# Two-part depth sum for an output projection, a half swap on the matrix engine, and a new order of one block's work in a fused attention and FFN kernel

## The chip, the cores and the metric

The kernel runs on one core of a Trainium2 chip. The metric is device microseconds of that core for one execution. The granted TensorE clock was 1.0 or within 0.4% of it. The span of a profile, from its first to its last instruction, is 1.8 to 1.9 us shorter than the time of the same run. A time is the median of several runs; every figure read from a trace is that of one profiled run. Engine names: PE is TensorE's matmul, PEld its weight load, DVE VectorE, ACT ScalarE, POOL GpSimd, SP SyncE.

## The reference

A lightning attention (causal, with a decay per head and a running state) is followed by a gated FFN. Cut to what matters:

```python
# q, k, v: (4, 8, 768, 64);  lam: (8,)
for b in range(nb):                                   # blocks of the sequence
    intra = einsum('bhic,bhjc->bhij', qb, kb) * Dmask         # scores times decay
    intra = einsum('bhij,bhjd->bhid', intra, vb)
    inter = einsum('bhid,bhde->bhie', qb * lam_pow, kv_state)
    out[:, :, sl] = intra + inter
    kv_state = lam_block * kv_state + einsum('bhsd,bhse->bhde', kb * rev_pow, vb)
x = out.transpose(0, 2, 1, 3).reshape(3072, 512)
y = (sigmoid(x @ w_gate) * (x @ w_val)) @ w_out               # 512 -> 1536 -> 512
```

## The kernel before

The sequence is cut into six blocks `n` of 128 positions for all four batches. A block has attention work (transposes `tk`, `tq`; scores `sp`; masked scores `MT`; outputs `op`, copied to `XT`; state sums `cp`, kept in `Sb`, from keys `kd` scaled by their decay) and FFN work: twelve column tiles `ft`, each with a gate product `gp` and a value product `vp`, whose gated result is `ht`, and a projection `po` of four row tiles. PE runs one program: attention of block n+1 is strewn between FFN products of block n, except at the start, where nothing can hide it. Weights arrive through POOL's DMA queue with a cast from float32 to bfloat16, between the loads of q, k and v. The parts that the change touches (cuts marked):

```python
    def load_gv(f0, f1):                       # gate and value weights of some column tiles
        fs = slice(f0 * 128, f1 * 128)
        nc.gpsimd.dma_start(out=WG[:, :, fs], in_=wg_r[:, :, fs])
        nc.gpsimd.dma_start(out=WV[:, :, fs], in_=wv_r[:, :, fs])
    def load_wo(c0, c1):                       # w_out by columns
        nc.gpsimd.dma_start(out=WO[:, :, c0:c1], in_=wo_r[:, :, c0:c1])
    ...
    def swap_halves():                         # the decay with its 64-row halves swapped
        for u in range(2):
            o, i = rows_of(u), rows_of(1 - u)
            nc.scalar.dma_start(out=lamq2[o, 1], in_=lamq2[i, 0])
            nc.scalar.dma_start(out=dec2[o, 1], in_=dec2[i, 0])
    ...
    def piece_po(n, tt, c0, c1, eng):          # projection of one row tile, full depth
        po = ps_ff.tile([128, DM], FP32, name="po", tag="ff")
        for ft in range(NFT):
            nc.tensor.matmul(po[:, :c1 - c0], lhsT=HT[n, ft][:, tt * 128:(tt + 1) * 128],
                             rhs=WO[:, ft, c0:c1], start=(ft == 0), stop=(ft == NFT - 1))
        ...                                    # copied to OB; stored at once if n > 0
    ...
    # end of block 0: projection by column halves, with block 1's attention between
    po(0, 0, m_(1, 1), kd(1, 4, 6, parts=[0]), c=cols[0])
    po(0, 1, pair(piece_c, 0, 0), pair(piece_c, 0, 1), kd(1, 6, 8, parts=[0]), c=cols[0])
    po(0, 2, trans(1, 1), c=cols[0])           # trans: k's and q's transposes together
    po(0, 3, pair(piece_s, 1, 1), m_(1, 2), m_(1, 3), kd(1, 0, 8, parts=[1]), att(1), c=cols[0])
    ...
            more[3].extend([lambda tt=tt: store(0, tt) for tt in range(B)])   # block 0's results
```

In `po(n, tt, *more)` the projection comes first and the listed pieces follow it.

Of the kernel before, what the change touches and what calls it, by code (L numbers as in the profile page):

```python
# [8 lines left out]
FP32 = mybir.dt.float32  # L9
# [7 lines left out]
def kernel(  # L17
# [65 lines left out]
    def load(n, what, b0=0, b1=B):  # L83
        sl = slice(n * C, (n + 1) * C)
        for c in what:
# [9 lines left out]
            if nat < b1:  # L95
                m = max(nat, b0)
                for u in range(2):
                    nc.gpsimd.dma_start(  # L98
                        out=T_[c, n][:, m:b1, u::2, :],
                        in_=src[m:b1, 1 - u::2, sl, :].rearrange("b h s d -> s (b h) d"))  # L100

    def load_gv(f0, f1):
        fs = slice(f0 * 128, f1 * 128)
        nc.gpsimd.dma_start(out=WG[:, :, fs], in_=wg_r[:, :, fs])  # L104
        nc.gpsimd.dma_start(out=WV[:, :, fs], in_=wv_r[:, :, fs])  # L105

    def load_wo(c0, c1):
        nc.gpsimd.dma_start(out=WO[:, :, c0:c1], in_=wo_r[:, :, c0:c1])

    KD = {}  # L110

# [23 lines left out]
    def load_hw(c, b, eng):  # L135
# [12 lines left out]
    nc.vector.memset(neg, 0.0)  # L148
    nc.vector.memset(tri, 0.0)
    make_identity(nc, ident, nomemset=True)  # L150
    nc.gpsimd.iota(dij, pattern=[[1, C]], base=0, channel_multiplier=-1,
                   allow_small_or_imprecise_dtypes=True)
    nc.gpsimd.affine_select(out=neg, in_=neg, compare_op=ALU.is_ge, fill=-30000.0, base=0,
# [13 lines left out]
    load(0, "v", 3, 4)  # L167
    for ft in range(4):
        load_gv(ft, ft + 1)
    load_gv(4, 6)  # L170

    lnl = const.tile([128, H], FP32, tag="lnl")
    nc.scalar.activation(lnl, lam_bc, AF.Ln)
    lnp = const.tile([128, HP], FP32, tag="lnp")
    for u in range(2):
        us = slice(u * 64, (u + 1) * 64)
        nc.scalar.activation(lnp[us, :], lam_bc[us, u::2], AF.Ln)
    lamq2 = const.tile([128, 2, HP, C], BF16, tag="lamq2")
    lamq, lamqs = lamq2[:, 0], lamq2[:, 1]
    for hp in range(HP):  # L180
        nc.scalar.activation(lamq[:, hp, :], ip1, AF.Exp, scale=lnp[:, hp:hp + 1])
    pk = const.tile([128, H], FP32, tag="pk")
    kds = const.tile([128, H], FP32, tag="kds")
    dec2 = const.tile([128, 2, HP], FP32, tag="dec2")
# [13 lines left out]
    def tables_late():  # L198
        nc.scalar.activation(pk, lnl, AF.Exp, scale=jn[:, 0:1])
        nc.scalar.activation(kds, lnl, AF.Exp, scale=jn[:, 1:2])  # L200
        nc.scalar.activation(dec, lnp, AF.Exp, scale=float(C))

    def swap_halves():
        for u in range(2):
            o, i = rows_of(u), rows_of(1 - u)
            nc.scalar.dma_start(out=lamq2[o, 1], in_=lamq2[i, 0])
            nc.scalar.dma_start(out=dec2[o, 1], in_=dec2[i, 0])

    def make_mask(u):
        nc.vector.tensor_tensor(  # L210
# [67 lines left out]

    def piece_i(n):
        for b in range(B):  # L280
            p, t = (ps_ff, "ff") if n == 1 and b < B - 1 else (ps_at, "ps")
            OP[n, b] = p.tile([128, HP, C], FP32, name="op", tag=t)
        for i in range(NB2):
            for hp in range(HP):
                for u, b in ((0, i), (1, NB2 - 1 - i), (0, NB2 + i), (1, B - 1 - i)):
                    w = u if b < NB2 else 1 - u
                    nc.tensor.matmul(OP[n, b][rows_of(w), hp, :], lhsT=Sb[rows_of(u), hp, b, :],  # L287
                                     rhs=QS[n, b][rows_of(u), hp, :],
                                     start=(hp == 0), stop=False, skip_group_check=True)
# [13 lines left out]
    def piece_x(n, bs, eng=None):  # L303
        if n not in XT:
            XT[n] = xtp.tile([128, NMT, B, C], BF16, tag="XT", name="XT")
        for b in bs:
            e = eng or (nc.vector if n < FIRST_XBAR and b % 2 else nc.scalar)
            (e.tensor_copy if e is nc.vector else e.copy)(XT[n][:, :, b, :], OP[n, b])  # L308

    def piece_c(n, hps):  # L310
        cp = ps_at.tile([128, len(hps), B, 64], FP32, name="cp", tag="ps")
        for i, hp in enumerate(hps):
            for b in range(B):
                for w in range(2):
                    h = 2 * hp + w
                    nc.tensor.matmul(cp[rows_of(half(b, h)), i, b, :],  # L316
                                     lhsT=KD[n][:, b, slot(n, b, h), :], rhs=T_["v", n][:, b, h, :],
                                     start=(i == 0 and b == 0), stop=(i == len(hps) - 1 and b == B - 1),
                                     skip_group_check=True)
        if n == 0:  # L320
            nc.vector.tensor_copy(Sb[:, hps[0]:hps[-1] + 1], cp)
            return
        for i, hp in enumerate(hps):
            for at, d in ((slice(0, NB2), dec), (slice(NB2, B), decs)):
                nc.vector.scalar_tensor_tensor(  # L325
                    out=Sb[:, hp, at, :], in0=Sb[:, hp, at, :], scalar=d[:, hp:hp + 1],
                    in1=cp[:, i, at, :], op0=ALU.mult, op1=ALU.add)
# [5 lines left out]
    def piece_gv(n, ft):  # L333
        fs = slice(ft * 128, (ft + 1) * 128)
        x = XT[n].rearrange("p m b c -> p m (b c)")
        gp = ps_ff.tile([128, TCH], FP32, name="gp", tag="ff")
        for mt in range(NMT):
            nc.tensor.matmul(gp, lhsT=WG[:, mt, fs], rhs=x[:, mt, :],  # L338
                             start=(mt == 0), stop=(mt == NMT - 1))
        sg = htp.tile([128, TCH], BF16, tag="sg", name="sg", bufs=3)  # L340
        nc.scalar.activation(sg, gp, AF.Sigmoid)  # L341
        vp = ps_ff.tile([128, TCH], FP32, name="vp", tag="ff")
        for mt in range(NMT):
            nc.tensor.matmul(vp, lhsT=WV[:, mt, fs], rhs=x[:, mt, :],  # L344
                             start=(mt == 0), stop=(mt == NMT - 1))
        HT[n, ft] = htp.tile([128, TCH], BF16, tag="ht", name="ht", bufs=2 * NFT)
        nc.vector.tensor_mul(HT[n, ft], sg, vp)  # L347

# [3 lines left out]
        nc.sync.dma_start(out=out[tt * S + n * C:tt * S + (n + 1) * C, c0:c1],  # L352
                          in_=OB[n, tt][:, c0:c1])

    def piece_po(n, tt, c0, c1, eng):
        if (n, tt) not in OB:
            OB[n, tt] = osb.tile([128, DM], FP32, tag="ob", name="ob")
        po = ps_ff.tile([128, DM], FP32, name="po", tag="ff")
        for ft in range(NFT):
            nc.tensor.matmul(po[:, :c1 - c0], lhsT=HT[n, ft][:, tt * 128:(tt + 1) * 128],  # L360
                             rhs=WO[:, ft, c0:c1], start=(ft == 0), stop=(ft == NFT - 1))
        o = OB[n, tt][:, c0:c1]
        (eng.copy if eng is nc.scalar else eng.tensor_copy)(o, po[:, :c1 - c0])  # L363
        if n:
            store(n, tt, c0, c1)

# [24 lines left out]
    tables_late()  # L391
    piece_s(0, [0])
    piece_m(0, 0)
    for b in range(2, 4):
        t_("k", 0, [b], ps_ff, "ff")
    e_k(0, [2])
    piece_s(0, [1])
    piece_m(0, 1)
    t_("q", 0, [2])
    e_q(0, [2], nc.scalar)  # L400
    e_k(0, [3])
# [10 lines left out]
    for b in range(3):  # L412
        piece_a(0, [b])
        piece_x(0, [b], nc.vector if b == 2 else nc.scalar)
    zeros(2)
    ops = [ps_at.tile([128, HP // 2, C], FP32, name="op", tag="ps") for _ in range(2)]
    for g in range(2):
        for hp in range(2 * g, 2 * g + 2):
# [3 lines left out]
                                 skip_group_check=True)  # L422
    nc.scalar.copy(XT[0][:, 0:2, 3, :], ops[0])
    nc.vector.tensor_copy(XT[0][:, 2:4, 3, :], ops[1])



    for n in range(2):
        make_kd(n)
    load_gv(6, 8)  # L430
    nc.gpsimd.dma_start(out=WG[:, :, 8 * 128:], in_=wg_r[:, :, 8 * 128:])
    for ft in (8, 10):
        fs = slice(ft * 128, (ft + 2) * 128)
        nc.gpsimd.dma_start(out=WV[:, :, fs], in_=wv_r[:, :, fs])  # L434
    load(1, "k", 0, 2)
    load(1, "q", 0, 2)
    load_wo(0, 256)
    load(1, "k", 2, 4)
    load(1, "q", 2, 4)
    load(1, "v", 0, 2)  # L440
    load(1, "v", 2, 4)
    load_wo(256, 512)
    load(2, "kq")

    gates = const.tile([128, 2], BF16, tag="gates")
# [19 lines left out]
    def gv(n, ft, *more):  # L465
        unit(lambda: piece_gv(n, ft), *more)

    def po(n, tt, *more, c=(0, DM), eng=nc.scalar):
        unit(lambda: piece_po(n, tt, *c, eng), *more)

    def pair(f, n, bp):
        return lambda: f(n, [2 * bp, 2 * bp + 1])
# [4 lines left out]
    def trans(n, bp):  # L477
        def go():
            bs = [2 * bp, 2 * bp + 1]
            t_("k", n, bs)  # L480
            e_k(n, bs)
            t_("q", n, bs)
            e_q(n, bs)
        return go

    def att(n):
        def go():
# [11 lines left out]
    behind = {ft: [] for ft in range(NFT)}  # L499
    for ft in range(4):  # L500
        behind[ft] = [kd(0, 2 * ft)]
    behind[0].append(swap_halves)
    behind[1].append(lambda: make_mask(0))
    behind[3].append(lambda: make_mask(1))
    behind[10] = [trans(1, 0), kd(1, 0, 2, parts=[0])]
    behind[11] = [pair(piece_s, 1, 0), m_(1, 0), kd(1, 2, 4, parts=[0])]
    for ft in range(NFT):
        gv(0, ft, *behind[ft])
    cols = [(256 * j, 256 * j + 256) for j in range(2)]
    po(0, 0, m_(1, 1), kd(1, 4, 6, parts=[0]), c=cols[0])  # L510
    po(0, 1, pair(piece_c, 0, 0), pair(piece_c, 0, 1), kd(1, 6, 8, parts=[0]), c=cols[0])
    po(0, 2, trans(1, 1), c=cols[0])
    po(0, 3, pair(piece_s, 1, 1), m_(1, 2), m_(1, 3), kd(1, 0, 8, parts=[1]), att(1), c=cols[0])

    for n in range(1, NSTEP):
        nx = n + 1
# [12 lines left out]
        if n == 1:  # L529
            more[4:11] = more[3:10]  # L530
            more[3] = []
            more[2].append(lambda: next_loads(2))
            more[3].extend([lambda tt=tt: store(0, tt) for tt in range(B)])
            more[8].append(lambda: next_loads(3))
        for ft in range(NFT):
            gv(n, ft, *more[ft])
            if (n, ft) == (1, 1):
                for tt in range(B):
                    po(0, tt, c=cols[1])
        for tt in range(B):  # L540
            if n == NSTEP - 1 and tt == B - 1:
                po(n, tt, c=(0, 384), eng=nc.vector)
# [39 lines left out]
```

## Time and profile before

The kernel took 229.48 us (median of 4 runs, 229.28 to 229.6).

| where PE loses time before block 1 | from, to (us) | lost (us) |
|---|---|---|
| value product of column tile 4, waiting for its weights | 22.32 to 23.74; products start 0.864 apart where nothing waits | 0.55 |
| projection 0, waiting for the first half of WO | 38.24 to 39.14 | 0.9 |
| last outputs of block 1, waiting for the last masked scores | 47.9 to 49.07 | 1.15 |
| first product of block 1, waiting for XT | 49.9 to 50.27 | 0.4 |

First the page of the kernel before: the span, then each engine's busy time with its share of the span and its count of instructions.

```profile
span 227.6 us, 4221 instructions
PE 217.2 (95%) x1688; PEld 110.4 (49%) x1712; DVE 102.3 (45%) x186; ACT 100.9 (44%) x216; POOL 61.6 (27%) x79
```

PE is the limit, so only its gaps can be won. The next fence is the timeline of PE in the kernel before: start, duration, engine, line, operation, result from operands, shape, count, and in brackets the idle time before it with what ended that.

```profile
22.32 1.03 PE L338 MATMUL gp<-XT,WG 128*128 128x512 bf16 x4
23.74 1.04 PE L344 MATMUL vp<-XT,WV 128*128 128x512 bf16 x4 [0.40 <-DMA WV<-in_moe_w_val_dram]
...
37.69 0.62 PE L267 MATMUL sp<-QS,KS 64*128 64x128 bf16 x16
39.14 2.78 PE L360 MATMUL po<-WO,ht 128*128 128x256 bf16 x24 [0.82 <-DMA WO<-in_moe_w_out_dram]
...
44.69 1.47 PE L360 MATMUL po<-WO,ht 128*128 128x256 bf16 x12
46.10 0.62 PE L267 MATMUL sp<-QS,KS 64*128 64x128 bf16 x16
...
49.07 0.41 PE L298 MATMUL op<-MT,vb 128*64 128x128 bf16 x8 [0.78 <-DVE MT L275]
49.29 0.70 PE L316 MATMUL cp<-vb,kd 128*64 128x64 bf16 x32
50.27 1.04 PE L338 MATMUL gp<-XT,WG 128*128 128x512 bf16 x3 [0.28 <-DVE XT L308]
```

The brackets name each wait. A bracket is somewhat shorter than the time lost, because a matmul's modelled end reaches past the start of the next. Scores of batches 2 and 3 (46.10) stand behind the fourth projection (44.69), and the masking of those scores on DVE takes 2.48 us, so the outputs at 49.07 have to wait. From there on PE is nearly full: blocks repeat every 34.6 us.

### The profile page before, as it was taken

The page shows a single profiled execution, that of the slowest core. Times are in us where ns is not written, and L with a number is a line of the kernel's source. Part 1 is how long each engine was busy: PE and PEld are TensorE (multiplying, and loading weights), DVE is VectorE, ACT ScalarE, POOL GpSimd, SP SyncE. Part 2 cuts the span into 40 slices and gives each one's busy share as a digit, 9 for nine tenths or more (in the row PEclk, how much of TensorE's full clock was granted, in tenths as well). Part 3 has the DMA queues.
Part 4 walks back from the last instruction along what each step waited for, and adds up shares of the span by engine and source line. Part 5 has one row for each costly group of instructions (what it writes and reads, how often), then busy time and mean ns, then how long its engine had stood idle before and what let it go on. Part 6 is the DMA issues. An engine that isn't in the chain of part 4 may idle for free.

```text
span 227.6 us, 4221 instructions
## 1 busy us (share of the span) xinstructions
PE 217.2 (95%) x1688; PEld 110.4 (49%) x1712; DVE 102.3 (45%) x186; ACT 100.9 (44%) x216; POOL 61.6 (27%) x79
## 2 busy tenths in 40 slices
PE   7799998989999999999999999999999999999994
PEld 2444345856644544444544444554444454444443
DVE  4764445584168530378530368630268600343300
ACT  5777335563337732328532338542433342434221
POOL 7999663900192058007600030000000000000000
PEclk9999999999999999999999999999999999999999
DMA  7999999999999949994992839002100012100022
GB/s 113 150 170 197 201 173 185 163 180 144 253 175 156 175 102 163 209 210 43 157 145 92 176 62 89 0 34 107 46 3 0 0 39 103 46 0 3 0 92 94
DMA packets 106195, 25.31 MB, mean 111 GB/s; under 512 B 96192, under 2 KB 103232, under 8 KB 106176
## 3 DMA queue, kind: packets, MB, share of 16 engines
q0 software_dynamic: 83392, 13.90, 79.7%
q1 hardware_dynamic: 22320, 11.01, 19.2%
q8 instruction: 13, 0.21, 0.4%
q10 hardware_dynamic: 464, 0.14, 0.3%
q14 instruction: 6, 0.05, 0.1%
HBM read 28.32 MB, written 6.29 MB: 152 GB/s over the span
## 4 chain that ended last, share of the span: by engine, by line
PE 79%; POOL 9%; DMA 7%; issue 2%; DVE 2%; ACT 0%; POOLq 0%
PE po L360 28%; PE vp L344 23%; PE gp L338 22%; DMA WO<-in_moe_w_out_dram 7%; PE sp L267 2%; POOL WG L104 2%; POOL WV L105 2%; PE op L298 2%; POOL qb L92 1%; POOL vb L92 1%; DVE MT L275 1%; PE op L287 1%; POOL kb L92 1%; PE cp L316 1%; POOL WV L434 1%
## 5 line engine op out<-in xcount | busy, mean ns | idle before, releaser
L347 DVE TENSOR_TENSOR ht<-sg,vp 128x512 bf16<-128x512 bf16 x72 | 49.4, 687 | 101.3 <-PE vp L344 99.7
L344 PE MATMUL vp<-XT,WV 128*128 128x512 bf16 x286 | 73.9, 379 | 0.8 <-DMA WV<-in_moe_w_val_dram 0.4
L338 PE MATMUL gp<-XT,WG 128*128 128x512 bf16 x273 | 71.9, 380 | 1.5 <-issue 0.5
L341 ACT ACTIVATE sg<-gp 128x512 bf16<-128x512 f32 x72 | 43.0, 597 | 65.8 <-PE gp L338 60.5
L360 PE MATMUL po<-WO,ht 128*128 128x512 bf16 (+3 forms) x343 | 63.6, 342 | 1.1 <-DMA WO<-in_moe_w_out_dram 0.8
L360 PEld LDWEIGHTS <-ht 128*128 128x128 bf16 x348 | 33.1, 98 | 29.4 <-issue 0.8
L344 PEld LDWEIGHTS <-WV 128*128 128x128 bf16 x288 | 28.0, 98 | 34.8 <-DMA WV<-in_moe_w_val_dram 1.2
L338 PEld LDWEIGHTS <-WG 128*128 128x128 bf16 x288 | 27.3, 98 | 32.9 <-DMA WG<-in_moe_w_gate_dram 0.6
L363 ACT COPY ob<-po 128x512 f32<-128x512 f32 (+2 forms) x28 | 14.4, 513 | 48.6 <-PE po L360 48.6
L275 DVE TENSOR_TENSOR MT<-sp,mask 128x512 bf16<-128x512 f32 x48 | 30.5, 683 | 2.0 <-PE sp L267 2.0
L120 ACT ACTIVATE kd<-kb,kds 128x128 bf16<-128x128 bf16 (+1 forms) x72 | 24.0, 403 | 0.0
L449 POOL COPY gates<-kt 128x1 bf16<-128x1 bf16 x4 | 0.7, 186 | 53.4 <-DMA kt<-kb 53.4
L92 POOL DMA_DIRECT2D vb<-in_v_dram x9 | 11.9, 1331 | 2.4 <-issue 1.3
L308 ACT CAST XT<-op 128x512 bf16<-128x512 f32 x20 | 10.3, 596 | 4.8 <-PE op L298 4.7
L325 DVE SCALAR_TENSOR_TENSOR Sb<-Sb,dec,cp 128x128 bf16<-128x128 bf16 x32 | 8.6, 341 | 3.3 <-PE cp L316 3.3
L98 POOL DMA_DIRECT2D qb<-in_q_dram x10 | 8.9, 911 | 2.2 <-DMA WG<-in_moe_w_gate_dram 1.7
L92 POOL DMA_DIRECT2D qb<-in_q_dram x8 | 9.1, 1135 | 0.8 <-POOLq L566 0.8
L98 POOL DMA_DIRECT2D kb<-in_k_dram x10 | 8.8, 894 | 0.8 <-DMA WV<-in_moe_w_val_dram 0.5
L373 PE MATMUL zps<-Sb 128*128 128x512 bf16 x18 | 6.8, 507 | 1.7 <-DVE Sb L147 1.5
L92 POOL DMA_DIRECT2D kb<-in_k_dram x6 | 7.0, 1162 | 3.3 <-DMA WO<-in_moe_w_out_dram 3.3
L298 PE MATMUL op<-MT,vb 128*64 128x128 bf16 x184 | 6.7, 221 | 0.8 <-DVE MT L275 0.8
L298 PEld LDWEIGHTS <-vb 128*64 128x64 bf16 x184 | 5.4, 110 | 1.7 <-issue 1.1
(57 smaller groups left out, 84.6 us busy)
## 6 DMA issues: line engine op xcount, KB each, us to landing
out_dram<-ob SPq DMA_DIRECT2D x23, 256.0 KB, 2.0
vb<-in_v_dram POOLq DMA_DIRECT2D x4, 512.0 KB, 7.0
qb<-in_q_dram POOLq DMA_DIRECT2D x6, 256.0 KB, 8.7
kb<-in_k_dram POOLq DMA_DIRECT2D x6, 256.0 KB, 7.5
qb<-in_q_dram POOLq DMA_DIRECT2D x12, 128.0 KB, 9.1
WO<-in_moe_w_out_dram POOLq DMA_DIRECT2D x2, 768.0 KB, 14.9
kb<-in_k_dram POOLq DMA_DIRECT2D x10, 128.0 KB, 8.6
WV<-in_moe_w_val_dram POOLq DMA_DIRECT2D x4, 256.0 KB, 9.0
```

The source lines that it names most:

```text
L92: nc.gpsimd.dma_start(out=T_[c, n][:, b0:nat], in_=src[b0:nat, :, sl, :].rearrange("b h s d -> s (b h) d"))
L98: nc.gpsimd.dma_start(out=T_[c, n][:, m:b1, u::2, :], in_=src[m:b1, 1 - u::2, sl, :].rearrange("b h s d -> s (b h) d"))
L120: nc.scalar.mul(KD[n][:, at, i, :], T_["k", n][:, at, i, :], kds[:, h:h + 1])
L275: nc.vector.tensor_tensor(out=MT[n, b][:, u], in0=SP[n, b][u], in1=(mask if n else mask0)[:, 1 - u if swapped(n, b) else u], op=ALU.mult)
L298: nc.tensor.matmul(OP[n, b][rows_of(w), hp, :], lhsT=T_["v", n][:, b, h, :], rhs=MT[n, b][:, slot(n, b, h) % 2, hp, :], start=(n == 0 and ...
L308: (e.tensor_copy if e is nc.vector else e.copy)(XT[n][:, :, b, :], OP[n, b])
L338: nc.tensor.matmul(gp, lhsT=WG[:, mt, fs], rhs=x[:, mt, :], start=(mt == 0), stop=(mt == NMT - 1))
L341: nc.scalar.activation(sg, gp, AF.Sigmoid)
L344: nc.tensor.matmul(vp, lhsT=WV[:, mt, fs], rhs=x[:, mt, :], start=(mt == 0), stop=(mt == NMT - 1))
L347: nc.vector.tensor_mul(HT[n, ft], sg, vp)
L360: nc.tensor.matmul(po[:, :c1 - c0], lhsT=HT[n, ft][:, tt * 128:(tt + 1) * 128], rhs=WO[:, ft, c0:c1], start=(ft == 0), stop=(ft == NFT - 1))
L363: (eng.copy if eng is nc.scalar else eng.tensor_copy)(o, po[:, :c1 - c0])
```

## The change

Its intent is to take away the gaps in the table. WO is loaded by depth (rows of 2 KB in memory) and projection 0 is summed in two halves of its depth, so that its first half needs only the first six depth tiles, in two loads. Weights of value tiles 4 and 5 come apart. The decay with swapped halves is no longer made by four DMAs: that of the positions in a block (`lamq`) comes from one PE product with a permuted identity, that of a whole block (`dec`) from the exponential that ACT runs anyway. Block 1's k transposes are parted from q's, and its scores of batches 2 and 3 go before the fourth projection. Product (1, 0) starts on batches 0 and 1 while the others are still copied. Cut to its core:

```diff
-    load_gv(4, 6)
+    load_g(4, 6)
+    load_v(4, 5)
+    load_v(5, 6)
...
     def swap_halves():
-        for u in range(2):
-            ...four DMAs issued by ACT...
+        ps = ps_at.tile([128, HP, C], FP32, name="lqs", tag="ps")
+        nc.tensor.matmul(ps, lhsT=swap, rhs=lamq, start=True, stop=True)
+        nc.vector.tensor_copy(lamqs, ps)
...
-    load_wo(0, 256)
+    load_wo(0, 3)                    # now depth tiles, all 512 columns
+    load_wo(3, 6)
...
-    load_wo(256, 512)
+    load_wo(6, 12)
...
+        if (n, ft) == (1, 0):        # gate and value product in two halves of the batches
+            parts = [slice(0, TCH // 2), slice(TCH // 2, TCH)]
...
-        for ft in range(NFT):
+        for ft in fts:
...
+        if fts[0]:                   # second half of the depth: added to the first
+            nc.vector.tensor_tensor(out=o, in0=o, in1=po[:, :c1 - c0], op=ALU.add)
...
-    po(0, 0, m_(1, 1), kd(1, 4, 6, parts=[0]), c=cols[0])
-    po(0, 1, pair(piece_c, 0, 0), pair(piece_c, 0, 1), kd(1, 6, 8, parts=[0]), c=cols[0])
-    po(0, 2, trans(1, 1), c=cols[0])
-    po(0, 3, pair(piece_s, 1, 1), m_(1, 2), m_(1, 3), kd(1, 0, 8, parts=[1]), att(1), c=cols[0])
+    po(0, 0, kd(1, 6, 8, parts=[0]), kd(1, 0, 2, parts=[1]), fts=lo)
+    po(0, 1, t_k(1, [2, 3]), kd(1, 2, 5, parts=[1]), fts=lo, eng=nc.vector)
+    po(0, 2, t_q(1, [2, 3]), pair(piece_c, 0, 0), pair(piece_c, 0, 1), kd(1, 5, 8, parts=[1]),
+       pair(piece_s, 1, 1), m_(1, 2), m_(1, 3), fts=lo)
+    po(0, 3, att(1), fts=lo)
...
-            more[3].extend([lambda tt=tt: store(0, tt) for tt in range(B)])
+            more[3].extend([lambda tt=tt, j=j: store(0, tt, 256 * j, 256 * j + 256)
+                            for tt in range(B) for j in range(2)])
```

Left out here: the scores of batch 1 of block 0 move ahead of two transposes; one filler matmul goes; the state sums of block 0 use other PSUM buffers and are copied by ACT instead of DVE; `piece_i` takes two more of its buffers from the pool of the scores; the XT copies of batches 1 and 2 change engines (DVE now has 2 and 3, ACT 0 and 1). PSUM is where the kernel puts PE's results. Block 0's results go out in eight stores instead of four.

## The prediction

> **What bounds it now.** The page gives TensorE (PE) 95% of a 227.6 us span at full clock; the chain of waits is 79% PE. From 90.9 us on a block takes 34.6 us, PE busy in 34.3 of it (windows); the diff touches nothing there. The timeline shows a weight product's four 128x512 matmuls in 0.864 us, 216 ns each; the Trainium skill ("TensorE: Matmul & The Clock Gate", Back-to-back issue gap) gives 512/2.4 + 2.5 ns: agreed, no product can shrink. Only gaps before 50.3 us are left (timeline of PE):
> - 15.38: first FFN product, after block 0's last v, landed about 14.6. The diff moves nothing on that path.
> - 22.32 to 23.74: the val product of column tile 4 waits for the two-tile WV load: 0.55 us lost.
> - 38.24 to 39.14: projection 0 waits for the first WO half: 0.9 us.
> - 46.1 to 50.27: block 1's scores stand behind the fourth projection, so their masks (DVE, 2.48 us) end at 49.01; PE waits 1.15 us for the last, then 0.4 us for the XT copies. Small waits: 0.3 us.
> Sum: 3.3 us.
>
> **What the change does.**
> 1. WV tile 4 alone is 128 KB, not 256: its packets end about 0.7 us sooner (690 packets of 256 B per us). The 0.55 us goes.
> 2. The half swap by PE is one matmul (0.22 us) where PE idles 0.35 us before 15.38, plus a DVE copy (0.65 us) in idle time. It removes four ACT-issued DMAs; between 20 and 23 us their 128 KB slow the POOL queue from 384 to 325 packets per us. The skill ("DMA: Bandwidth & Descriptors", Issuing engines are not separate DMA queues) says they share engines; this trace agrees. What is queued behind lands about 0.4 us sooner.
> 3. WO by depth: 1 KB packets move 207 GB/s against 197 for 512 B, so 2 KB rows alone give 0.2 us. What counts is that three depth tiles land first: the projection starts on them near 37.7, and the next three land near 38.2, when wanted. The 0.9 us goes nearly whole.
> 4. Scores of batches 2 and 3 go before the fourth projection: the mask wait drops to about 0.1 us. New: they wait 0.3 us for DVE's scaled q, transposed just before; and ACT gets the state copies (2 x 0.6 us) and finishes last: chain kd, ob, Sb, kd, ob, XT ends near 47.7. PE would be ready at 47.4.
> 5. Product (1,0) in two halves starts on batches 0 and 1; no added streaming. The projection's later halves cost PE the same 5.2 us; the adds (DVE, about 0.69 us each) fit under 1.3 us.
>
> So block 1's first product should start near 47.8 instead of 50.3, all critical, and this 2.5 us should carry to the end.
>
> **Prediction: 227.0 us**, 8 in 10 between 225.8 and 228.5. Faster by over 2%: 0.04; within 2%: 0.95; slower: 0.01.
>
> **Right or wrong in the profile.** First product still near 15.4; no WV wait near 23; WO waits under 0.3 us; scores of batches 2, 3 before the fourth projection; first block-1 product at 47.3 to 48.5; blocks from 90 us on still 34.6 us.
>
> **What would make it wrong.** ACT later than I add up (no pause from 39 to 47.7), moving the wait to XT; WO's second piece landing after 38.5, because one more DMA per queue delays issue; block 2's transposed q (landed 61.9 us) wanted before it lands, giving part back; the prologue moving with its reordering.

## More of the kernel before

Last, the end of the program, in the timeline of all engines in the kernel before.

```profile
222.70 2.73 SPq L352 DMA_DIRECT2D out_dram<-ob  x3
224.03 0.56 DVE L363 COPY ob<-po 128x384 f32<-128x384 f32 x1 [8.96 <-PE po L360]
224.70 0.27 ACT L363 COPY ob<-po 128x128 f32<-128x128 f32 x1 [2.03 <-PE po L360]
```

The last copy ends at 224.97 and SP's last store is over at 222.70 + 2.73 = 225.43. The last matmul ends at 224.67, so the tail, from there to the end of the span at 227.63, is 2.96 us.

## The result, and the profile after

The changed kernel took 228.0 us (median of 4 runs, 227.9 to 228.09), the kernel before 229.48. The ratio is 0.9937, with an interval of 0.9919 to 0.9954: 0.6% faster, within 2%. A ratio here is the mean time of one kernel's fast runs over that of the other's of the same rounds, so it is not quite the ratio of the medians.

The timeline of PE in the changed kernel, for the stretch shown of before:

```profile
22.12 1.03 PE L353 MATMUL gp<-XT,WG 128*128 128x512 bf16 x4
22.98 1.03 PE L353 MATMUL vp<-XT,WV 128*128 128x512 bf16 x4
...
37.02 0.62 PE L276 MATMUL sp<-QS,KS 64*128 64x128 bf16 x16
37.58 3.02 PE L381 MATMUL po<-WO,ht 128*128 128x512 bf16 x12
40.85 0.61 PE L233 MATMUL tk<-ident,kb 128*128 128x128 bf16 x8 [0.25 <-DMA kb<-in_k_dram]
41.29 1.46 PE L381 MATMUL po<-WO,ht 128*128 128x512 bf16 x6
...
43.98 0.62 PE L276 MATMUL sp<-QS,KS 64*128 64x128 bf16 x16 [0.16 <-DVE QS L243]
44.53 1.47 PE L381 MATMUL po<-WO,ht 128*128 128x512 bf16 x6
...
46.50 1.08 PE L307 MATMUL op<-MT,vb 128*64 128x128 bf16 x32
47.42 0.67 PE L326 MATMUL cp<-vb,kd 128*64 128x64 bf16 x32
48.08 0.60 PE L353 MATMUL gp<-XT,WG 128*128 128x256 bf16 x4
```

The waits for WV, for the first of WO, for the last mask and for XT are gone. In their place are a wait for the keys (0.25 us before 40.85) and one for DVE's scaled q (0.16 us). There is a third, hidden inside the piece at 37.58: its third matmul starts at 38.02 and its fourth at 38.49, where the others follow each other by 0.216 us. That is a stop of 0.26 us, until the second piece of WO is there (landed at 38.45). The wait for the keys, too, costs more than its bracket: from 40.43, when the next matmul could have started, to 40.85 it is 0.42 us. The first product of block 1 starts at 48.08 instead of 50.27, which is 2.19 us sooner.

That lead is still there at the last matmul: it ends at 222.43 instead of 224.67, 2.24 us sooner. But the span is only 1.56 us shorter (226.07 and 227.63). So 0.68 us were lost after the last matmul. The timeline of the end of the changed kernel:

```profile
221.79 0.56 DVE L387 COPY ob<-po 128x384 f32<-128x384 f32 x1 [8.96 <-PE po L381]
222.38 1.19 SPq L373 DMA_DIRECT2D out_dram<-ob  x2
222.46 0.27 ACT L387 COPY ob<-po 128x128 f32<-128x128 f32 x1 [2.03 <-PE po L381]
```

The copies stand as they did in relation to the last matmul, but the last store is over at 222.38 + 1.19 = 223.57, which is 0.84 us after the last copy ended (222.73). Before, this was 0.46 us. No code of the end of the program was changed.

Reading SP's own instructions one by one out of the trace, semaphore waits included, shows where the time is. The number counts SP's recorded instructions from the start of the program, and the gap is the time since the instruction before it ended.

```text
kernel before                                  changed kernel
no.  start   gap   what                        no.  start   gap   what
78   225.00  0.04  wait, own semaphore         79   222.76  0.04  wait, own semaphore
79   225.06  0.04  last store                  80   223.24  0.46  last store
80   225.89  0.46  check 1 of 9                81   223.63  0.05  check 1 of 9
81   225.97  0.06  check 2                     82   223.69  0.04  check 2
88   226.75  0.19  check 9 (last store)        89   225.19  0.90  check 9 (last store)
```

In both kernels SP's 80th instruction stands still for 0.46 us. The semaphore that the last store waits for in the changed kernel (ACT's copy) was up at 222.74, so at 223.24 it was not waiting for that. Before, the 80th was the first check after the last store, and its standstill lay inside the 1.67 us in which that store landed. In the changed kernel, the 80th is the last store itself, so the standstill delays it. In both traces an 8 KB packet of the kind "instruction" on DMA queue 14 follows the standstill by 0.6 to 0.8 us (at 226.66 before, 223.86 after). In the changed kernel it falls into the transfer of the last store, and the last of this store's 16 parts lands 0.31 us after the fifteenth (0.02 us before).

### The profile page after: what moved, and what is told of

The parts are those of the page before. It is cut to its first block, busy times and chain, and to the rows that moved or that the text cites. A ratio compares the mean times of both kernels' runs of the same rounds, so it can differ in the third digit from the quotient of the medians.

```text
span 226.1 us, 4168 instructions
## 1 busy us (share of the span) xinstructions
PE 218.4 (97%) x1672; PEld 106.6 (47%) x1672; DVE 105.3 (47%) x192; ACT 101.2 (45%) x215; POOL 62.9 (28%) x81
## 3 DMA queue, kind: packets, MB, share of 16 engines
q1 hardware_dynamic: 22896, 11.01, 20.1%
## 4 chain that ended last, share of the span: by engine, by line
PE 80%; DMA 9%; POOL 8%; issue 1%; DVE 0%; ACT 0%; POOLq 0%
PE po L381 27%; PE gp L353 23%; PE vp L353 23%; DMA kb<-in_k_dram 5%; DMA WG<-in_moe_w_gate_dram 4%; POOL WV L106 2%; PE op L307 2%; PE sp L276 2%; POOL WG L103 2%; POOL vb L92 1%; PE op L296 1%; POOL qb L92 1%; PE cp L326 1%; POOL kb L92 1%; DVE QS L243 0%
## 5 line engine op out<-in xcount | busy, mean ns | idle before, releaser
L353 PE MATMUL gp<-XT,WG 128*128 128x512 bf16 (+1 forms) x292 | 74.2, 376 | 0.0
L353 PE MATMUL vp<-XT,WV 128*128 128x512 bf16 (+1 forms) x292 | 74.1, 376 | 0.0
L381 PE MATMUL po<-WO,ht 128*128 128x512 bf16 (+2 forms) x300 | 63.9, 371 | 0.1
L381 PEld LDWEIGHTS <-ht 128*128 128x128 bf16 x300 | 28.4, 98 | 32.6 <-issue 0.4
L353 PEld LDWEIGHTS <-WG 128*128 128x128 bf16 x292 | 27.8, 98 | 32.2 <-DMA WG<-in_moe_w_gate_dram 0.4
L387 ACT COPY ob<-po 128x512 f32<-128x512 f32 (+1 forms) x23 | 13.1, 571 | 41.2 <-PE po L381 39.2
L106 POOL DMA_DIRECT2D WV<-in_moe_w_val_dram x9 | 7.1, 808 | 0.0
```

The source lines that it names most:

```text
L106: nc.gpsimd.dma_start(out=WV[:, :, f0 * 128:f1 * 128], in_=wv_r[:, :, f0 * 128:f1 * 128])
L353: nc.tensor.matmul(ps[:, part], lhsT=W[:, mt, fs], rhs=x[:, mt, part], start=(part is parts[0] and mt == 0), stop=(part is parts[-1] and m ...
L387: (eng.copy if eng is nc.scalar else eng.tensor_copy)(o, po[:, :c1 - c0])
```

## The experiments

Eleven kernels ran, in three groups, with five rounds each. The kernel before had medians of 229.68, 229.71 and 229.61 us in these groups. All results were correct. "Tail" is the time from the end of the last matmul to the end of the span, and "product" is the start of the first product of block 1.

| run | median us | ratio to before (interval) | product | last matmul ends | tail |
|---|---|---|---|---|---|
| kernel before | 229.48 | 1 | 50.27 | 224.67 | 2.96 |
| changed kernel | 228.00 | 0.9937 (0.9919 to 0.9954) | 48.08 | 222.43 | 3.65 |
| a_whole | 227.83 | 0.9925 (0.9911 to 0.9940) | 48.03 | 222.38 | 3.49 |
| b_split | 229.87 | 1.0012 (0.9997 to 1.0026) | 50.16 | 224.56 | 3.25 |
| a_late_scores | 229.21 | 0.9981 (0.9968 to 0.9995) | 49.46 | 223.80 | 3.77 |
| a_cols | 228.42 | 0.9952 (0.9937 to 0.9967) | 48.45 | 222.85 | 3.58 |
| a_quarters | 227.02 | 0.9896 (0.9881 to 0.9911) | 47.79 | 222.13 | 3.01 |
| a_one_v | 228.25 | 0.9936 (0.9924 to 0.9948) | 47.93 | 222.28 | 3.62 |
| a_dma_swap | 228.10 | 0.9934 (0.9921 to 0.9947) | 48.66 | 223.01 | 3.29 |
| a_nohalf | 228.77 | 0.9959 (0.9947 to 0.9971) | 49.01 | 223.35 | 3.60 |
| a_best | 227.44 | 0.9905 (0.9892 to 0.9918) | 48.15 | 222.49 | 2.98 |
| a_joined | 227.86 | 0.9923 (0.9911 to 0.9935) | 47.99 | 222.34 | 3.63 |
| b_five | 230.66 | 1.0047 (1.0034 to 1.0061) | 49.95 | 224.34 | 3.99 |

Products of kernels that share all code up to there scatter by up to 0.3 us from profile to profile (changed kernel, a_whole, a_quarters: 48.08, 48.03, 47.79; kernel before, b_split, b_five: 50.27, 50.16, 49.95). Differences smaller than that are not read as effects. Part of the scatter is there early. The weights of value tile 2, on which no edit of these runs bears, landed between 18.95 and 19.42 us in the thirteen traces (landings are read from the semaphore updates), and in a_late_scores, a_nohalf and a_dma_swap, where they were late, the rest of the queue was late too.

### The tail

**a_whole**: the changed kernel, with four whole stores again.

```diff
-            more[3].extend([... store(0, tt, 256 * j, 256 * j + 256) for tt in range(B) for j in range(2)])
+            more[3].extend([lambda tt=tt: store(0, tt) for tt in range(B)])
```

> The changed kernel, but block 0's results are stored in 4 whole stores (512 columns) instead of 8 half ones. The last matmul of the changed kernel ends 2.24 us earlier than that of the kernel before, but the span is only 1.5 us shorter: the tail after the last matmul is 3.67 us instead of 2.96. Theory A: the four added store instructions shift SP's instruction stream, so that an 8 KB instruction fetch falls onto the last store. Then the tail returns to about 2.96 us and the time to about 227.3 us. Rival B: the tail has nothing to do with the number of stores (other parts of the change, or chance): tail 3.67, time 228.0 us.

The tail was 3.49 us, between the two theories, and the time 227.83 us. The last store was issued promptly again (0.07 us after the copy), and its parts landed together. But the 80th instruction was now one of the closing checks: it stood still 0.46 us, partly after the store had landed (224.43), so that this check began only at 224.71. It is the check of the last store itself, which had moved to a semaphore that is checked fifth of nine; four more checks, about 0.065 us each, came after it. So theory A was right about the standstill and wrong that undoing the stores would clear the tail.

**b_split**: the kernel before, with eight half stores, the reverse edit.

> The kernel before with block 0's 4 stores made 8 half ones, nothing else. Theory A (the added stores lengthen the tail): last matmul still at about 224.7 us, tail 3.7 instead of 2.96 us, time about 230.2 us. Rival B: tail stays 2.96 us and the time 229.5 us.

The tail was 3.25 us and the time not distinguishable from the kernel before. Here the 80th instruction was an earlier store, and its standstill lay in SP's idle time. Of the 0.29 us more, 0.25 came after the landing: the last store was again checked fifth, at 226.68, and the checks behind it followed. The expected 0.7 us did not come, so the number of stores is not in itself the cause. What counts is where the 80th instruction falls, and which semaphore the last store holds.

**a_quarters**: still more stores, placed by these two rules. The changed kernel, with sixteen quarter stores.

```diff
-            more[3].extend([... store(0, tt, 256 * j, 256 * j + 256) for tt in range(B) for j in range(2)])
+            more[3].extend([... store(0, tt, 128 * j, 128 * j + 128) for tt in range(B) for j in range(4)])
```

> The changed kernel, but block 0's results go out in 16 quarter stores (128 columns) instead of 8 half ones: more transfers, not fewer. In all six traces so far SP's 80th instruction stands still for 0.44 to 0.46 us with nothing to wait for, and 0.6 to 0.8 us later an 8 KB packet of instructions is moved. In the changed kernel the 80th is the last store. Theory: eight more stores move the 80th into the idle time before the last store, and leave the last store on the semaphore that is checked last: issue within 0.1 us of the copy, landing in about 1.7 us, tail about 2.95 us, time about 227.3 us, although more stores are made. Rival (more stores cost more at the end): tail 3.7 us or more, time 228.0 us or more.

In five of the six traces named there the standstill can be seen; in b_split the 80th instruction falls into idle time, which hides it. The theory held. SP in this run:

```text
no.  start   gap   what
79   191.67  2.19  store of block 4
80   192.45  0.45  wait, own semaphore      (packet of instructions at 193.3)
81   214.98  22.52 store of block 5
89   222.51  0.03  last store               (copy ended 222.44, landed 224.22)
```

The standstill lies in 22 us of idle time, the last store holds the semaphore that is checked last, the tail is 3.01 us and the time 227.02 us. Its interval (0.9881 to 0.9911) lies wholly below that of the changed kernel (0.9919 to 0.9954): with twice as many stores it has the lowest time. Of the 0.98 us between the two medians, the traces put 0.64 us in the tail. The last matmul also ended 0.29 us sooner, which is within the scatter and not an effect of the stores. The end of its timeline, where the two stores are over at 222.90, 0.46 us after the last copy, as in the kernel before:

```profile
221.50 0.56 DVE L387 COPY ob<-po 128x384 f32<-128x384 f32 x1 [8.96 <-PE po L381]
222.09 0.81 SPq L373 DMA_DIRECT2D out_dram<-ob  x2
222.17 0.27 ACT L387 COPY ob<-po 128x128 f32<-128x128 f32 x1 [2.04 <-PE po L381]
```

**b_five**: the kernel before with one of four stores cut in two.

```diff
-            more[3].extend([lambda tt=tt: store(0, tt) for tt in range(B)])
+            more[3].extend([lambda: store(0, 0, 0, 256), lambda: store(0, 0, 256, 512)])
+            more[3].extend([lambda tt=tt: store(0, tt) for tt in range(1, B)])
```

> The kernel before with one of block 0's four stores cut in two, one SP transfer more, to test the tail's cause with everything else as before. Theory: SP's 80th instruction, which in the kernel before was the first check after the last store, is then the last store itself (0.45 us stall exposed), and the last store moves to a semaphore that is checked second, so that seven more checks of 0.065 us follow its landing: tail 3.9 to 4.2 us instead of 2.96, time 230.5 us or more. Rival: the tail stays near 3.0 us, time 229.7 us.

One more store made the kernel before 0.5% slower: 230.66 us, tail 3.99 us. The 80th was the semaphore wait directly before the last store, not the store itself, with the same effect: 0.45 us, and the store was issued 0.51 us after the copy. The packet of instructions fell into the landing again (last part 0.19 us after the fifteenth), and the checks that followed the landing took about 0.45 us. PE's work was not touched: its last matmul ended at 224.34.

In all thirteen traces the 80th instruction of SP stands still for 0.44 to 0.46 us, except in b_split, where it falls into an idle stretch and no standstill can be told apart, and an instruction packet follows. In each trace where the packet's time falls into the transfer of the last store, one part of that store lands 0.19 to 0.46 us after the others (the changed kernel, a_late_scores, a_cols, a_one_v, a_nohalf, a_joined, b_five). In the other six, the last part comes within 0.04 us. That the packet is the refill of SP's own instructions follows from this timing alone; the trace does not say whose instructions a packet holds.

### The order of the scores

**a_late_scores**: the changed kernel, with block 1's scores of batches 2 and 3 behind the fourth projection.

```diff
     po(0, 2, t_q(1, [2, 3]), pair(piece_c, 0, 0), pair(piece_c, 0, 1), kd(1, 5, 8, parts=[1]),
-       pair(piece_s, 1, 1), m_(1, 2), m_(1, 3), fts=lo)
-    po(0, 3, att(1), fts=lo)
+       fts=lo)
+    po(0, 3, pair(piece_s, 1, 1), m_(1, 2), m_(1, 3), att(1), fts=lo)
```

> The changed kernel, but block 1's scores of batches 2 and 3 go after the fourth projection, as in the kernel before. Theory: this order made most of the gain in block 1: PE waits about 1 us for the last mask again, the first product of block 1 starts near 49.1 instead of 48.09 us, time about 229.0 us. Rival: the gain is the earlier WO alone, and the order is worth under 0.3 us: time under 228.3 us.

The product was 1.38 us later and the time 229.21 us, so most of the gain needs this order. But 0.28 us of the 1.38 came before the order could act: the keys' transposes started at 41.13 instead of 40.85, since the queue was late already at 19 us (value tile 2 landed at 19.39 instead of 19.12). From these transposes to the product it is 8.33 us instead of 7.23, so the order is worth 1.10 us. The timeline of PE in this run:

```profile
41.13 0.61 PE L233 MATMUL tk<-ident,kb 128*128 128x128 bf16 x8 [0.26 <-DMA kb<-in_k_dram]
...
45.57 0.62 PE L276 MATMUL sp<-QS,KS 64*128 64x128 bf16 x16
46.12 0.24 PE L296 MATMUL op<-QS,Sb 64*64 64x128 bf16 x2
46.75 0.21 PE L296 MATMUL op<-QS,Sb 64*64 64x128 bf16 x1 [0.38 <-DVE MT L284]
47.34 0.60 PE L296 MATMUL op<-QS,Sb 64*64 64x128 bf16 x29 [0.38 <-DVE MT L284]
```

The wait came in another place than expected. The inter-block outputs at 46.12 read no mask at all, and yet they wait for DVE's masking: it frees the PSUM buffers of the scores, which these outputs take. In the kernel before, three of the four outputs used the other pool, and PE stopped later, at the outputs that do read the mask. So this run undoes the order under the new assignment of buffers; the order alone under the old one was not tried.

### WO by depth

**a_cols**: the changed kernel, with WO loaded and projection 0 summed by halves of its columns.

```diff
-    load_wo(0, 3)
-    load_wo(3, 6)
+    nc.gpsimd.dma_start(out=WO[:, :, 0:256], in_=wo_r[:, :, 0:256])
...
-    lo, hi = range(NFT // 2), range(NFT // 2, NFT)
+    lo, hi = [(256 * j, 256 * j + 256) for j in range(2)]      # passed as c= instead of fts=
```

> The changed kernel, but WO is loaded and projection 0 is done in two halves of columns, as before, all else as changed. Theory: the projection waits again for all of the first 768 KB (from 37.6 to about 38.6 us), but most of that is covered by the wait for k, which ends at 40.8 us anyway, so the first product of block 1 is only about 0.35 us later, time about 228.35 us. Rival (the prediction's step 3): the whole 0.9 us comes back, time about 228.9 us.

The timeline of PE in this run:

```profile
38.56 2.78 PE L381 MATMUL po<-WO,ht 128*128 128x256 bf16 x24 [0.89 <-DMA WO<-in_moe_w_out_dram]
44.33 0.62 PE L276 MATMUL sp<-QS,KS 64*128 64x128 bf16 x16 [0.16 <-DVE QS L243]
```

The whole wait of about 0.9 us is back at the projection, but the wait for the keys no longer shows, and the product comes only 0.37 us later (48.45). That is what the theory said. The depth split won 0.98 us at the start of the projection (37.58 instead of 38.56) and gave most of it back: 0.26 us in the stop for WO's second piece and 0.42 us in the wait for the keys, which stand behind WO in the same queue.

### The value weights, the swap, the halves

**a_one_v**: value tiles 4 and 5 in one load again.

```diff
-    load_g(4, 6)
-    load_v(4, 5)
-    load_v(5, 6)
+    load_gv(4, 6)
```

> The changed kernel, but WV tiles 4 and 5 come in one load again. Theory: PE waits about 0.5 us for it near 23 us, so the projection starts near 38.0 instead of 37.58, but there and before the keys' transposes it then waits less for data that land at 38.5 and 40.8 us anyway; the first product of block 1 is at most 0.15 us later, time about 228.1 us. Rival (the prediction's step 1, waits add up): 0.5 us later, time 228.5 us.

Theory held. The product at 23.44 was 0.34 us late (it could have followed the one at 22.24 after 0.864 us; the bracket in PE's timeline says 0.18), the projection started at 37.95, and the product of block 1 came at 47.93, no later than in the changed kernel. The time, 228.25 us, has the same ratio within its interval. The split of this load is therefore worth nothing in the time.

**a_dma_swap**: the halves swapped by four ACT-issued DMAs behind the first product, as before.

```diff
-        ps = ps_at.tile([128, HP, C], FP32, name="lqs", tag="ps")
-        nc.tensor.matmul(ps, lhsT=swap, rhs=lamq, start=True, stop=True)
-        nc.vector.tensor_copy(lamqs, ps)
+        for u in range(2):
+            o, i = rows_of(u), rows_of(1 - u)
+            nc.scalar.dma_start(out=lamq2[o, 1], in_=lamq2[i, 0])
+            nc.scalar.dma_start(out=dec2[o, 1], in_=dec2[i, 0])
...
-    swap_halves()
...
+    behind[0].append(swap_halves)
```

> The changed kernel, but the decay halves are swapped by four ACT-issued DMAs again. Theory (step 2): the queue behind is slowed by about 0.4 us, so the second piece of WO and the keys land that much later; PE waits for both; first product of block 1 near 48.45 instead of 48.09 us, time about 228.35 us. Rival: the queue has slack enough, nothing lands later: time 228.0 us.

The time says "rival": 228.10 us. The profile says the opposite. Counting packets between 20 and 23 us, POOL's queue moved 157 KB per us in this run, 187 in the changed kernel and 167 in the kernel before. The second piece of WO landed at 39.08 (38.45 in the changed kernel) and the keys at 41.29 (40.71). The timeline of PE has:

```profile
18.13 1.04 PE L354 MATMUL vp<-XT,WV 128*128 128x512 bf16 x4 [0.31 <-DMA WV<-in_moe_w_val_dram]
41.43 0.61 PE L234 MATMUL tk<-ident,kb 128*128 128x128 bf16 x8 [0.20 <-DMA kb<-in_k_dram]
```

The product is 0.58 us later. A part of this is chance: the wait at 18.13 also appeared in a_late_scores, a_nohalf and a_best, which have no such DMAs, and value tile 2 landed 0.18 us late (19.30 instead of 19.12) before the four DMAs moved, from 20.1 to 22.3 us. By the landing of value tile 5 the queue was 0.63 us late (24.02 instead of 23.39), and so was WO's second piece. That leaves about 0.45 us for the DMAs, and about 0.40 us at the product. The time hides this loss because the tail is 0.36 us shorter: the edit changed SP's instruction stream too (97 recorded instructions instead of 94), the 80th instruction fell into idle time, and the last store was issued 0.09 us after its copy, though it was checked fifth.

**a_nohalf**: product (1, 0) in one piece.

```diff
-        if (n, ft) == (1, 0):
+        if False:
             parts = [slice(0, TCH // 2), slice(TCH // 2, TCH)]
```

> The changed kernel, but product (1,0) is not halved. The XT copies end at 48.7 us, PE is free at about 48.05. Theory (step 5): first product of block 1 near 48.75 instead of 48.09 us, time about 228.6 us. Rival: the copies are in time and the halves are worth nothing: time 228.0 us.

As expected: 228.77 us. The timeline of PE in this run:

```profile
49.01 1.04 PE L353 MATMUL gp<-XT,WG 128*128 128x512 bf16 x3 [0.66 <-DVE XT L317]
```

The halves save this wait of 0.66 us for DVE's copies. The rest of the 0.93 us between 49.01 and 48.08 lies earlier: the scores of batches 2 and 3 started 0.26 us later in this run, whose queue was late by 0.30 us at value tile 2 already.

### The parted transposes, and a try for more

**a_joined**: k's and q's transposes of batches 2 and 3 together behind the third projection.

```diff
-    po(0, 1, t_k(1, [2, 3]), kd(1, 2, 5, parts=[1]), fts=lo, eng=nc.vector)
-    po(0, 2, t_q(1, [2, 3]), pair(piece_c, 0, 0), ...
+    po(0, 1, kd(1, 2, 5, parts=[1]), fts=lo, eng=nc.vector)
+    po(0, 2, t_k(1, [2, 3]), t_q(1, [2, 3]), pair(piece_c, 0, 0), ...
```

> The changed kernel, but block 1's transposes of k and q (batches 2 and 3) stand together behind the third projection. Theory: PE no longer waits 0.25 us for the keys, but ACT copies them 1.5 us later, so the scores start 0.2 to 0.3 us later, first product of block 1 near 48.3 us, time about 228.2 us: parting the transposes is worth little. Rival: parting them is what makes room for the scores before the fourth projection: product 0.7 us or more later, time 228.7 us.

The wait for the keys went and one of 0.34 us for ACT's copy of them came. The scores started at 43.89 (43.98), the product at 47.99, and the time was 227.86 us. Parting the transposes is worth nothing here; the expected small loss did not come either.

**a_best**: quarter stores, and state sums and q's transposes moved behind the second projection.

```diff
-    po(0, 1, t_k(1, [2, 3]), kd(1, 2, 5, parts=[1]), fts=lo, eng=nc.vector)
-    po(0, 2, t_q(1, [2, 3]), pair(piece_c, 0, 0), pair(piece_c, 0, 1), kd(1, 5, 8, parts=[1]),
-       pair(piece_s, 1, 1), m_(1, 2), m_(1, 3), fts=lo)
+    po(0, 1, t_k(1, [2, 3]), pair(piece_c, 0, 0), pair(piece_c, 0, 1), t_q(1, [2, 3]),
+       kd(1, 2, 5, parts=[1]), fts=lo, eng=nc.vector)
+    po(0, 2, kd(1, 5, 8, parts=[1]), pair(piece_s, 1, 1), m_(1, 2), m_(1, 3), fts=lo)
```

> The changed kernel with quarter stores, and with the state sums and the transposes of q moved from behind the third projection to behind the second (keys, state sums, q), so that the 0.7 us in which DVE scales q lies under the third projection. Theory (block 1 then waits for PE's own order, not for data): scores of batches 2 and 3 start near 43.7 without the 0.16 us wait, and end the block 0.3 to 0.4 us sooner: time about 226.65 us, below the 227.0 us of quarter stores alone. Rival: keys and q land too late for it (keys near 40.8 us, q about 1 us later), PE waits for them instead: time 227.0 us or more.

This fell short: 227.44 us, not better than a_quarters (0.9905 and 0.9896, intervals overlap). The keys came at 40.9, q caused no wait, and the scores started at 44.05, 3.13 us after the keys' transposes: exactly the distance of the changed kernel (43.98 and 40.85). The wait for the scaled q was gone, but the same pieces took longer in this order: from start to start, transposes of k 0.54 us, state sums 0.75, transposes of q 0.44, projection 1.40, where the changed kernel has 0.44 for k, 1.30 for the projection, 0.54 for q and 0.85 for the state sums with the wait of 0.16. Why was not looked into.

## Why the prediction was right or wrong

The time, 228.0 us, lay inside the range of 225.8 to 228.5 and the class (within 2%) was the likeliest one. The gain was 1.5 us where 2.5 was predicted; that the time was still inside is owed to the width of the range, not to a tail that was foreseen.

- **First FFN product near 15.4, unchanged.** Right. It started at 15.14, but the kernel before had it at 15.38, 15.11 and 15.06 in three profiles and the changed kernel and its variants at 15.00 to 15.46, so there is no effect.
- **Step 1, WV.** The wait went, but a_one_v shows that the time does not notice, since later landings in the same queue decide.
- **Step 2, the swap.** The mechanism was right, and the size too: 0.4 us predicted, and with the DMAs back the second piece of WO and the keys came 0.6 us later, of which about 0.45 us arose while the DMAs moved. The Trainium skill ("DMA: Bandwidth & Descriptors", Issuing engines are not separate DMA queues) says that DMAs of all issuing engines share the same DMA engines; the queue's 187 and 157 KB per us agree.
- **Step 3, WO.** Larger rows moved 200 packets of 1 KB per us, 205 GB/s, against 381 to 389 of 512 B, 195 to 199 GB/s, so little, as said. "The 0.9 us goes nearly whole" was too much: the second piece came at 38.45 instead of 38.2, which left 0.26 us of wait, and 0.42 us for the keys followed, a wait that the prediction had not seen. Against column halves the step gained 0.37 us in all.
- **Step 4, the scores.** Right in its main part: the mask wait went, and the order is worth 1.1 us in a_late_scores. The scores started near 44.0. The prediction had ACT finish 0.3 us after PE was ready (47.7 and 47.4). The trace shows no such wait: ACT stood idle for 0.33 us before each of its last two groups of copies, its XT copies ended at 48.03, and the product at 48.08 stands without a wait behind the state sums.
- **Step 5, the halves.** Right: 0.66 us of wait without them.
- **First product of block 1** near 47.8, in a range of 47.3 to 48.5: it started at 48.08. A gain of 2.2 us was left of 2.5; the two waits of step 3 (0.26 and 0.42 us) are where it fell short.
- **"This 2.5 us should carry to the end."** This is the step that failed. The 2.2 us reached the last matmul whole (2.24), and then 0.68 us were lost behind it: 0.42 in the issue of the last store and 0.26 in its landing. The prediction named four ways to be wrong, and the end of the program was not among them, because no line of it is changed. The runs showed that four more stores at 60 us move SP's 80th instruction, the one that stands still, onto the last store at 222 us; with four stores again (a_whole) it falls onto a closing check and still costs a part.

The parts do not add up exactly. The order (1.10), the halves (0.66), the depth split (0.37) and the swap (0.40) make 2.5 us where the product gained 2.2; the landings scatter by 0.3 us, and the parts may share waits.

What stays open: what the standstill of the 80th instruction consists of, and what the changes of buffers and copying engines are worth, which no run took back alone.

## What to carry to other kernels

Compare two traces at the last matmul and at the end of the span, not only by their times: a change in one engine's number of instructions cost or saved 0.3 to 1 us at the end in these runs, and it hid the loss in the time of a_dma_swap. Where a small time matters, look at which instruction of the storing engine falls onto the last store and in which order the final checks come; a harmless split of an earlier store moves both. And when several loads share a queue, removing the wait for one of them only shows the next: read the landing of everything that follows before adding the waits up.

## What the Trainium skill lacked or had wrong

- "Runtime: NRT & Kernel Launch", Instruction fetch mechanics, says that a boundary in the instruction stream costs "one DMA tail-bump, mostly hidden", and gives blocks of 16 KiB. Here the fetches of queue 14 came as packets of 8192 bytes (queue 8 had packets of 16384 bytes), and SP stood still for 0.44 to 0.46 us at its 80th recorded instruction, 0.6 us or more before such a packet. It was hidden in the kernel before, in a_quarters, a_best, a_dma_swap and b_split, and exposed in whole or part in the other eight traces. That this standstill is such a boundary follows from the timing alone.
- "DMA: Bandwidth & Descriptors", Queues, rings and completion order, gives queue row 14 to the runtime's own traffic, refills among it, which agrees with the kind "instruction" on queue 14. Its paragraph on arbitration has each DMA engine take the queue rows in turn, a packet at a time, but gives no figure for what an instruction packet costs a transfer in flight: in the seven traces where they met, one part of the last store landed 0.19 to 0.46 us after the others.
- No page read here mentions the closing checks: nine semaphore waits in a fixed order, about 0.065 us each, so that a last transfer on a semaphore checked fifth, or second, of nine cost 0.25 or 0.45 us more than on the one checked last (after the landing of the last store, the span went on for 0.90 us in the kernel before, 1.15 in b_split and 1.35 in b_five).
